# A linear-attention and feed-forward kernel: 96-partition loads and a fixed instruction order in place of scheduled 128-token tiles

## The chip, the cores and the metric

The kernel runs on one core of one Trainium2 chip. The metric is the device time of one execution in microseconds (us), the median of the runs. Profiles are of one execution each, and times inside a profile count from the start of its span. "Matmul" is one TensorE instruction; ACT is ScalarE, DVE is VectorE, POOL is GpSimd, SP is the engine whose queue issues the DMAs, and PEld is the loading of stationary operands.

## The reference

Eight batches, eight heads, 576 tokens, head size 64. Attention without a score matrix feeds a feed-forward block that has no nonlinearity besides one product:

```python
q_s = exp(q - max) / sum over d          # per token and head
k_s = exp(k - max) / sum over tokens     # per head and channel
kv  = einsum('bhsd,bhse->bhde', k_s, v)
x   = einsum('bhsd,bhde->bhse', q_s, kv) # then (b, s, h*64): 4608 tokens x 512
a, b = x @ w1, x @ w2                    # 512 -> 1024 each
out = ((a * b) @ w3) @ w_out             # 1024 -> 1024 -> 512
```

Both kernels fold `w3 @ w_out` into one 1024 x 512 matrix first ("the fold"), so a chunk of 512 tokens costs 64 matmuls in the first stage (a and b, 8 groups of 8) and 32 in the second stage, all with 512 columns. There are 9 chunks. Attention of a batch must be done before the chunks that use its tokens.

## The kernel before

Tokens are loaded in tiles of 128 (four, and one of 64), so that each DMA moves runs of 64 floats, 256 bytes. Every tile gets its own exponential, reduction, normalisation on GpSimd, and one transpose per pair of heads:

```python
for st in range(N_ST):                       # 5 token tiles
    nc.sync.dma_start(out=q32[:ns], in_=q[b, :, s0:s0 + ns, :].transpose([1, 0, 2]))
    # ... k32, v32 the same way
    nc.scalar.activation(out=eq[:ns], in_=q32[:ns], func=AF.Exp)
    # ... ek, v16, dsum, dsr
    nc.gpsimd.tensor_tensor(out=eqn[:ns], in0=eq[:ns],
                            in1=dsr[:ns, :, None].broadcast_to([ns, H, D]), op=ALU.mult)
for p in range(NPAIR):
    # ... kv matmuls over the 5 tiles, two casts into kv2
    for st in range(N_ST):
        nc.tensor.transpose(tpq[:, st, :ns], eqns[st][:ns, 2*p:2*p+2, :]..., ident[:ns, :ns])
    # ... scale by rc on the way to qsT, then x = kv2.T @ qsT (512 + 64 columns)
```

Weights come through two staging buffers and ACT casts. The order of instructions on each engine is left to the tile scheduler; the program is emitted as whole blocks:

```python
attention_batch(0); load_w12(); attention_batch(1); load_w3o(); attention_batch(2)
for j in range(N_CHUNK):
    ffn_chunk(j)
    if j + 3 < B:
        attention_batch(j + 3)
```

The softmax here doesn't subtract the row's maximum and nothing guards it: scores larger than these inputs give would overflow.

## Time and profile before

| | before |
|---|---|
| time | 317.44 us (316.34 to 318.54) |
| span of the profile | 315.9 us |
| TensorE busy | 84% |
| first second-stage matmul (end of the fold) | 101.9 us |
| period of a chunk with attention (second stages of chunks 3 to 6 start at 162.33, 192.55, 221.78, 252.48) | 30.0 us |
| chunk without attention (second-stage starts at 284.2 and 304.9) | 20.8 us |

From the page of the kernel before: the span in 40 slices (7.9 us each), tenths of busy time, granted TensorE clock, DMA share, and GB/s; then the chain that ended last, by engine and by line.

```profile
PE   0128479398999999999989999988898989999995
PEclk9999999855999999999999999999999999999999
DMA  9995799346999499993695478458844402002003
GB/s 172 218 245 192 224 236 220 114 175 200 227 234 212 135 220 215 259 199 67 182 224 113 100 214 178 91 125 226 166 102 100 149 3 100 33 2 101 33 0 133
...
PE 64%; POOL 9%; ACT 8%; DMA 7%; DVE 5%; issue 3%; SPq 2%; POOLq 0%; DVEq 0%; ACTq 0%
```

The start is poor in TensorE work up to about 70 us, with the DMA engines full in five of nine slices at only 172 to 245 GB/s, and two slices (63 to 79 us) near half clock. After that TensorE looks full. It is not: the profile draws a 512-column matmul 0.38 us long although the next one can start 0.216 us after it, so a gap shorter than the difference is not seen as idle. The waits of TensorE between 130 and 230 us (in all, times, longest):

```profile
PE pt L169 <- POOL eqn L149: 7.2, 12, 1.0
```

Then two extracts of the timeline, each with a single transpose between dense matmuls (start, duration, engine, line, operation, operands); above the second, ACT's copy of x out of the PSUM buffer that the transposes share:

```profile
151.16 0.38 PE L206 MATMUL po<-W3O_579,ab 128*128 128x512 f16 x1
151.38 0.22 PE L169 MATMUL pt<-ident,eqn 128*128 128x128 f16 x1
151.43 0.38 PE L206 MATMUL po<-W3O_580,ab 128*128 128x512 f16 x1
```

```profile
120.50 0.23 ACT L182 ACTIVATE xT_102<-pt 128x64 f16<-128x64 f32 x1
120.44 0.38 PE L206 MATMUL po<-W3O_577,ab 128*128 128x512 f16 x1
120.78 0.22 PE L169 MATMUL pt<-ident,eqn 128*128 128x128 f16 x1
120.84 0.38 PE L206 MATMUL po<-W3O_578,ab 128*128 128x512 f16 x1
```

Dense matmuls start 0.216 us apart. The transpose at 151.38 waited for nothing: 0.27 us lie between the starts of its neighbours, so it cost 0.056 us. The one at 120.78 had 0.40 us between its neighbours, 0.13 us of that a wait, too short for the waits view: ACT freed the single PSUM buffer (`pt`) only at 120.73. Of the twenty single 128-column transposes between dense matmuls from 110 to 255 us, only four cost no more than 0.056 us. Twelve transposes between 130 and 230 us waited up to 1.0 us for GpSimd, and the dense matmuls behind them, for which the trace shows no wait of their own, started 0.06 to 0.13 us later.

### The profile page before, as it was taken

The numbers are of one execution on the slowest core, as the hardware profiler recorded it, in microseconds if no ns is written. First come the engines' busy times: TensorE is split into PE (matmuls) and PEld (weight loads), VectorE is DVE, ScalarE is ACT, GpSimd is POOL, SyncE is SP. The second block draws the span as 40 slices with busy tenths as digits, with TensorE's granted clock in tenths as the row PEclk, the third lists the DMA queues.
The fourth block names the chain that finished last, engine by engine and source line by source line (L and its number), as shares of the span: only waits on it lengthen the run. The fifth ranks groups of instructions, "written<-read, shape, count | busy, mean of one in ns | idle before, by whom it ended". The sixth has DMA issues, their size and how long they took to land.

```text
span 315.9 us, 4080 instructions
## 1 busy us (share of the span) xinstructions
PE 264.9 (84%) x1376; PEld 119.9 (38%) x1376; DVE 147.2 (47%) x364; ACT 133.3 (42%) x249; POOL 66.1 (21%) x104
## 2 busy tenths in 40 slices
PE   0128479398999999999989999988898989999995
PEld 0014024144545454335344434444354335444441
DVE  1234024442444485457546645664465447344342
ACT  3336544454865254245343625344433531430320
POOL 4441022400214212422322242132304240000000
PEclk9999999855999999999999999999999999999999
DMA  9995799346999499993695478458844402002003
GB/s 172 218 245 192 224 236 220 114 175 200 227 234 212 135 220 215 259 199 67 182 224 113 100 214 178 91 125 226 166 102 100 149 3 100 33 2 101 33 0 133
DMA packets 121172, 48.49 MB, mean 154 GB/s; under 512 B 113472, under 2 KB 113472, under 8 KB 121152
## 3 DMA queue, kind: packets, MB, share of 16 engines
q1 hardware_dynamic: 121152, 48.25, 66.3%
q8 instruction: 10, 0.16, 0.2%
q14 instruction: 10, 0.08, 0.1%
HBM read 38.80 MB, written 9.44 MB: 153 GB/s over the span
## 4 chain that ended last, share of the span: by engine, by line
PE 64%; POOL 9%; ACT 8%; DMA 7%; DVE 5%; issue 3%; SPq 2%; POOLq 0%; DVEq 0%; ACTq 0%
PE pab L195 18%; PE po L206 15%; PE pab L190 14%; POOL eqn L149 9%; PE pkv L158 5%; PE pt L169 5%; ACT bsb L199 4%; PE po L119 3%; PE px L178 2%; DMA q_173<-in_q_dram 2%; DVE dsum L144 2%; DMA w_716<-in_moe_w_dram 2%; DMA q_207<-in_q_dram 2%; DMA w_352<-in_moe_w_dram 1%; DVE osb L209 1%
## 5 line engine op out<-in xcount | busy, mean ns | idle before, releaser
L201 DVE TENSOR_TENSOR ab<-pab,bsb 128x512 f16<-128x512 f32 x72 | 49.7, 690 | 79.5 <-ACT bsb L199 78.6
L199 ACT CAST bsb<-pab 128x512 f16<-128x512 f32 x72 | 42.1, 585 | 103.8 <-PE pab L195 103.7
L149 POOL TENSOR_TENSOR eqn<-eq,dsr 128x512 f16<-128x512 f16 (+1 forms) x40 | 41.6, 1041 | 177.6 <-DVE dsr L147 67.1
L169 PE MATMUL pt<-ident,eqn 128*128 128x128 f16 (+1 forms) x160 | 22.8, 233 | 26.8 <-POOL eqn L149 25.8
L209 DVE COPY osb<-po 128x512 f32<-128x512 f32 x36 | 24.8, 690 | 25.6 <-PE po L206 25.4
L206 PEld LDWEIGHTS <-ab 128*128 128x128 f16 x288 | 25.3, 98 | 28.3 <-issue 1.4
L144 DVE TENSOR_REDUCE dsum<-eq 128x8 f32<-128x512 f16 (+1 forms) x40 | 27.1, 676 | 17.9 <-ACT eq L137 17.8
L169 PEld LDWEIGHTS <-eqn 128*128 128x128 f16 (+1 forms) x160 | 14.2, 103 | 53.6 <-POOL eqn L149 41.4
L190 PE MATMUL pab<-xT_102,w_0_3_350 128*128 128x512 f16 x72 | 28.3, 396 | 3.2 <-ACT w_0_3_350 L93 2.6
L190 PE MATMUL pab<-xT_101,w_0_2_342 128*128 128x512 f16 x72 | 28.3, 396 | 1.8 <-ACT w_0_2_342 L93 1.2
L195 PE MATMUL pab<-xT_99,w_1_0_330 128*128 128x512 f16 x72 | 28.2, 392 | 1.1 <-ACT bsb L199 1.1
L195 PE MATMUL pab<-xT_102,w_1_3_354 128*128 128x512 f16 x72 | 28.1, 390 | 1.0 <-ACT w_1_3_354 L93 1.0
L190 PE MATMUL pab<-xT_100,w_0_1_334 128*128 128x512 f16 x72 | 28.3, 396 | 0.6 <-ACT xT_100 L181 0.6
L190 PE MATMUL pab<-xT_99,w_0_0_326 128*128 128x512 f16 x72 | 28.5, 396 | 0.0
L195 PE MATMUL pab<-xT_101,w_1_2_346 128*128 128x512 f16 x72 | 28.1, 390 | 0.3 <-ACT w_1_2_346 L93 0.3
L195 PE MATMUL pab<-xT_100,w_1_1_338 128*128 128x512 f16 x72 | 28.1, 390 | 0.0
L173 DVE TENSOR_SCALAR qsT<-pt,rc 128x512 f16<-128x512 f16 x32 | 15.5, 484 | 16.3 <-PE pt L169 15.9
L158 PEld LDWEIGHTS <-ek 128*128 128x128 f16 (+1 forms) x160 | 13.5, 103 | 22.0 <-ACT ek L139 5.9
L206 PE MATMUL po<-W3O_576,ab 128*128 128x512 f16 x36 | 13.7, 380 | 0.0
L206 PE MATMUL po<-W3O_580,ab 128*128 128x512 f16 x36 | 13.7, 380 | 0.0
L206 PE MATMUL po<-W3O_575,ab 128*128 128x512 f16 x36 | 13.7, 380 | 0.0
L206 PE MATMUL po<-W3O_578,ab 128*128 128x512 f16 x36 | 13.7, 380 | 0.0
(284 smaller groups left out, 392.8 us busy)
## 6 DMA issues: line engine op xcount, KB each, us to landing
out_dram<-osb SPq DMA_DIRECT2D x36, 256.0 KB, 2.6
w_324<-in_moe_w_dram SPq DMA_DIRECT2D x1, 512.0 KB, 5.0
w_328<-in_moe_w_dram SPq DMA_DIRECT2D x1, 512.0 KB, 5.8
w_332<-in_moe_w_dram SPq DMA_DIRECT2D x1, 512.0 KB, 3.3
w_336<-in_moe_w_dram SPq DMA_DIRECT2D x1, 512.0 KB, 3.3
w_340<-in_moe_w_dram SPq DMA_DIRECT2D x1, 512.0 KB, 3.2
w_344<-in_moe_w_dram SPq DMA_DIRECT2D x1, 512.0 KB, 3.4
w_348<-in_moe_w_dram SPq DMA_DIRECT2D x1, 512.0 KB, 3.6
```

The costliest lines, as they stand in the source:

```text
L119: nc.tensor.matmul(wps, lhsT=w3Tf[:, gt * P:(gt + 1) * P], rhs=wosb[gt], start=(gt == 0), stop=(gt == N_FT - 1))
L144: nc.vector.tensor_reduce(out=dsum[:ns], in_=eq[:ns], axis=mybir.AxisListType.X, op=ALU.add)
L149: nc.gpsimd.tensor_tensor(out=eqn[:ns], in0=eq[:ns], in1=dsr[:ns, :, None].broadcast_to([ns, H, D]), op=ALU.mult)
L158: nc.tensor.matmul(kvp[:, 0:129], lhsT=eks[st][:ns, p * P:(p + 1) * P], rhs=v16s[st][:ns, p, 0:129], start=(st == 0), stop=(st == N_ST - 1))
L169: nc.tensor.transpose(tpq[:, st, :ns], eqns[st][:ns, 2 * p:2 * p + 2, :].rearrange("a h d -> a (h d)"), ident[:ns, :ns])
L173: nc.vector.tensor_scalar(out=qsT[:, 0:512], in0=tpq[:, 0:4, :], scalar1=rc, scalar2=None, op0=ALU.mult)
L190: nc.tensor.matmul(pa, lhsT=w1sb[ct][:, fb * P:(fb + 1) * P], rhs=xT[ct][:, t0:t0 + 512], start=(ct == 0), stop=(ct == N_CT - 1))
L195: nc.tensor.matmul(pb, lhsT=w2sb[ct][:, fb * P:(fb + 1) * P], rhs=xT[ct][:, t0:t0 + 512], start=(ct == 0), stop=(ct == N_CT - 1))
L199: nc.scalar.copy(out=bsb, in_=pb)
L201: nc.vector.tensor_tensor(out=ab, in0=pa, in1=bsb, op=ALU.mult)
L206: nc.tensor.matmul(po, lhsT=abT[ft][:, tb * P:(tb + 1) * P], rhs=W3O[ft], start=(ft == 0), stop=(ft == N_FT - 1))
L209: nc.vector.tensor_copy(out=osb, in_=po)
```

## The change

The intent: longer DMA runs, fewer and larger operations, and an order of instructions written by hand. Tokens are taken as 96 partitions x 6 consecutive tokens, so that a run is 1536 bytes and half a batch of q, k or v is one DMA of 576 KB; nine staging slots instead of a few; weights w1 and w2 arrive in column quarters, so that the first groups can start early; the scale moves from q to kv. Attention's PSUM buffers change too: three that all its pieces share, in place of one each for kv, for x and for the transposes (with the end of x); and the weight casts are spread over ACT, VectorE and GpSimd. The output rows are permuted back by the store. The guard `manual_schedule()` keeps every engine in the order in which the program emits.

```diff
+    R = 6
+    SP = S // R                                     # 96 partitions
+    stage = ctx.enter_context(tc.tile_pool(name="stage", bufs=9))
+    def load_qkv(b, which, hf):
+        t = slot([SP, 4, R * D])
+        nc.sync.dma_start(out=t, in_=src[b, 4*hf:4*hf+4].rearrange("h (p r) d -> p h (r d)", r=R))
+    def piece_t(b, p):                              # 6 transposes, one copy
+    def piece_kv(b, g):                             # 12 matmuls; kv2 scaled by rc here
+    def piece_x(b, p):                              # 2 matmuls of 288 columns, ACT copies
+    order = ctx.enter_context(tc.manual_schedule())
 ...
+    elementwise(1, 1)
+    pc = pieces(1)
+    for tb in range(4):
+        s2(0, tb)                                   # second stage of chunk 0, with its stores
+        for f in ((1, 0, 2), (3, 4, 5), (6, 7), (8, 9))[tb]:
+            pc[f]()
+    for which in "kvq":
+        load_qkv(2, which, 1)
+    elementwise(2, 0)                               # k exp, v cast, q exp, reduction, normalisation
+    elementwise(2, 1)
+    for hf in range(2):
+        for which in "kvq":
+            load_qkv(3, which, hf)
+    for j in range(1, N_CHUNK):                     # one piece and one elementwise step
+        for i, (kind, n) in enumerate(seq):         # after each group
+            if kind == "g": s1(j, n)
+            elif j > 1:     s2(j - 1, n)
+            if i < len(pc): pc[i]()
+            if i < len(ew): ew[i]()
+            if i >= 4 and i - 4 < len(ld): load_qkv(j + 3, *ld[i - 4])
 ...
-    for j in range(N_CHUNK):
-        ffn_chunk(j)
-        if b < B: attention_batch(b)
```

## The prediction

> **What bounds it now.** TensorE. In the timeline's last two chunks, where only FFN is left, one 512-token chunk (96 matmuls of 512 columns) takes 20.8 us (second-stage starts at 284.2 and 304.9), 0.216 us per matmul. The Trainium skill ("TensorE: Matmul & The Clock Gate", Back-to-back issue gap) gives about 216 ns for N=512; the trace agrees. FFN needs 9 x 20.8 = 187 us; folding w3 into w_out 64 x 0.216 + 64 transposes = about 18 us; attention about 4.5 us per batch. Together about 241 of the 316 us span; some 75 us are lost, in two places:
> - Start, 0 to 102 us. The first second-stage matmul is at 101.8 us in the chain. Batch 0's 256-byte packets keep the DMA engines full (share 1.0 to 1.3) for 180 to 220 GB/s; 4 KB weight rows move 158 GB/s at share 0.54, so about 290 GB/s when full. The Trainium skill ("DMA: Bandwidth & Descriptors", Specifications) asks for at least 512 B per transfer; the trace agrees. Weights come through two staging buffers: each load waits for an ACT cast (1.05 us) and its own 3.3 us to landing. From 60 to 80 us the granted clock is 0.55 to 0.6.
> - Steady state. A chunk with attention takes about 29 us against 20.8 + 4.5. The waits view shows TensorE held by the GpSimd normalisation (7.2 us between 130 and 230), because transposes stand singly in TensorE's order ahead of matmuls that were ready.
>
> **What the change does.**
> - 1536-byte runs, 6 loads per batch instead of 15, nine staging slots: batch 0 (3.5 MB) lands by about 14 us, w1/w2 by 28, w_out by 35, w3 by 49 (estimate at 290 to 300 GB/s). Chunk 0's first stage starts at about 22 us and runs dense (14 us); the fold, 2.3 us per row block, ends at about 57 us instead of 101.
> - Hand order: attention pieces come as bursts between dense groups, normalised a chunk ahead, so TensorE should hardly wait. Each chunk with attention: 20.8 + about 5.6 us.
> - Added: 24 + 24 small matmuls per batch instead of 20 + 20, about 0.1 us each; two 288-column matmuls instead of 512 + 64: about +1 us per batch on TensorE. More output DMAs (split at 96 rows), off the chain. DVE per chunk (12 x 0.69, 4 reductions of about 0.95, copies) about 16 us of 26; ACT about 15; GpSimd about 11: none binds. Moving the scale to kv saves small DVE operations, nothing on the chain.
>
> **Sum.** Fold ends at 57; second stage of chunk 0 with attention 1: 12.5 plus 1 to 2 us waiting for batch 1's loads, to 71; chunk 1 first stage with attention 2: 19.4, to 90; chunks 2 to 6: 5 x 26.4, to 222; chunks 7, 8: 41.6; last second stage 6.9; eviction and output DMA 4 (as now). About 275 us of span, plus 1.5 (time over span now): **276 us, range 264 to 290**. Faster by over 2%: 0.96; within 2%: 0.03; slower: 0.01.
>
> **Right if:** first second-stage matmul at 53 to 62 us; first-stage start at 19 to 26; chunk period with attention 25.5 to 28; GpSimd nearly gone from the chain, TensorE over 80% of it; no 256-byte packets, 280 GB/s or more at the start; last two chunks unchanged.
>
> **Wrong if:** in-order ACT or DVE delays first-stage evictions (exponentials of 0.85 us queue before them), so that three PSUM buffers run out and the period is 28 or more; GpSimd contends with DVE; the start is limited by casts or slots, not bandwidth, and the fold ends after 65 us; half clock after stalls in the fold; or small matmuls cost more than 0.1 us in bursts.

## The result

| | before | after |
|---|---|---|
| time | 317.44 us | 291.35 us (290.51 to 292.19) |
| ratio | | 0.916 (0.908 to 0.924) |
| first stage of chunk 0 | scattered, from 24.8 us | dense, from 27.2 us |
| first second-stage matmul | 101.9 us | 70.4 us |
| period of a chunk with attention | 30.0 us | 24.14 us |
| last second stage with store | about 11 us | about 11.5 us |

Ratios here are the mean time of one kernel's fast runs over that of the other's in the same rounds, so they are not quite the ratios of the medians quoted beside them. The change is faster by 8%, but 15 us short of the forecast of 276.

The same lines of the page of the changed kernel (slices of 7.3 us):

```profile
PE   0218997739693399999999999999999999999993
PEclk9999999998888579999999999999999999999999
DMA  7999999990139999949946965971121112121124
GB/s 182 254 326 391 357 351 282 261 250 15 41 97 236 256 256 256 228 118 220 280 129 156 257 149 128 261 208 38 48 62 38 36 47 64 36 73 38 55 76 121
...
PE 79%; DMA 8%; ACT 5%; DVE 3%; issue 1%; SPq 1%; DVEq 0%; ACTq 0%
```

From about 106 us on TensorE has no hole. Before that there are deep ones around 62 us and from 87 to 102 us, a smaller one around 76 us, reduced clock in several slices, and, at 65 to 87 us, three slices in which the DMA engines do almost nothing (15, 41, 97 GB/s) in a kernel that is waiting for data.

Extracts of the chain of the changed kernel in order of time, from the end of the fold on (start, length, what):

```profile
61.07 1.57 ACT ek L111 x2
62.65 1.47 ACT eq L120 x2
64.11 0.94 ACT w_611 L232
65.10 1.03 PE att L235 x8
...
86.21 1.19 ACT ek L111 x2
87.40 9.72 DMA st<-in_q_dram
97.20 1.58 ACT eq L120 x2
99.29 1.86 PE pab L204 x4
```

Two stops stand out. In the fold, TensorE's last transposes wait for a cast of w3 (w_611) that stands behind four exponentials on ACT. In chunk 1, TensorE waits until 99.29 us for something that begins with a load. ACT's own timeline and SP's show how (the bracket is the engine's idle time before the row and what ended it):

```profile
86.07 1.59 ACT L111 ACTIVATE ek<-st 96x768 f16<-96x768 f32 x2
87.55 1.58 ACT L120 ACTIVATE eq<-st 96x768 f16<-96x768 f32 x2
92.55 1.58 ACT L111 ACTIVATE ek<-st 96x768 f16<-96x768 f32 x2 [3.43 <-DMA st<-in_k_dram]
97.20 1.58 ACT L120 ACTIVATE eq<-st 96x768 f16<-96x768 f32 x2 [3.07 <-DMA st<-in_q_dram]
98.68 0.56 ACT L201 CAST a_880<-pab 128x512 f16<-128x512 f32 x1
...
76.37 9.92 SPq L224 DMA_DIRECT2D out_dram<-osb  x8
86.39 0.37 SPq L78 DMA_DIRECT2D st<-in_k_dram  x1
86.88 0.41 SPq L78 DMA_DIRECT2D st<-in_v_dram  x1
87.40 0.42 SPq L78 DMA_DIRECT2D st<-in_q_dram  x1
```

The first-stage copy a_880 needs nothing but a matmul that ended at about 87 us. It runs at 98.68 us, because eight exponentials of batch 2 come before it on ACT, four of them wait for loads, and those loads were issued only at 86.4 us, after the eight stores of chunk 0's second stage had gone through the same SP queue. The Trainium skill ("TensorE: Matmul & The Clock Gate", the specification table's row Engine queue depth) calls the queues of ScalarE, VectorE and GpSimd strict FIFO; this trace agrees, with a ready copy of 0.56 us held for some 11 us.

Two more losses of chunk 1 do not stand out in the chain. TensorE waited 3.9 us, until 91.38 us, for GpSimd's normalised tile of batch 2: the exponentials before it (86.07 and 87.55) were emitted only after chunk 0's second stage, although their loads had landed by 66.8 us (experiment 6 moves them, and this wait goes). And after the stops TensorE ran slowly: from 91.9 to 105.3 us its 512-column matmuls started 0.43 us apart in place of 0.216 (granted clock 0.50 from 94 to 102 us), which cost an estimated 3.6 us, by these distances.

### The profile page after: what moved, and what is told of

Same layout as the page of the kernel before. It is cut to its first block, busy times and chain, and to the rows that moved or that the text cites. A ratio compares the mean times of both kernels' runs of the same rounds, so it can differ in the third digit from the quotient of the medians.

```text
span 290.4 us, 3985 instructions
## 1 busy us (share of the span) xinstructions
PE 245.5 (85%) x1440; PEld 125.1 (43%) x1440; DVE 140.0 (48%) x268; ACT 124.3 (43%) x217; POOL 79.2 (27%) x64
## 2 busy tenths in 40 slices
DMA packets 31443, 48.49 MB, mean 167 GB/s; under 512 B 2240, under 2 KB 24768, under 8 KB 31424
## 4 chain that ended last, share of the span: by engine, by line
PE 79%; DMA 8%; ACT 5%; DVE 3%; issue 1%; SPq 1%; DVEq 0%; ACTq 0%
PE pab L204 22%; PE pab L198 21%; PE po L215 21%; DMA st<-in_q_dram 8%; PE po L243 5%; PE att L152 4%; PE att L180 3%; PE att L169 2%; ACT eq L120 2%; ACT ek L111 1%; PE att L235 1%; DVE ds L134 1%; SPq L78 1%; DVE osb L218 0%; ACT w_542 L232 0%
## 5 line engine op out<-in xcount | busy, mean ns | idle before, releaser
L138 POOL TENSOR_TENSOR eqn<-eq,dr 96x768 f16<-96x768 f16 x32 | 46.8, 1470 | 98.9 <-DVE dr L136 57.5
L134 DVE TENSOR_REDUCE ds<-eq 96x12 f32<-96x768 f16 x32 | 30.0, 936 | 44.2 <-ACT eq L120 44.1
L215 PEld LDWEIGHTS <-abT 128*128 128x128 f16 x288 | 27.6, 99 | 30.5 <-issue 1.1
L218 DVE TENSOR_SCALAR osb<-po 128x512 f32<-128x512 f32 x36 | 24.8, 688 | 27.2 <-PE po L215 26.2
L120 ACT ACTIVATE eq<-st 96x768 f16<-96x768 f32 x32 | 26.4, 843 | 11.8 <-DMA st<-in_q_dram 11.8
L111 ACT ACTIVATE ek<-st 96x768 f16<-96x768 f32 x32 | 25.8, 843 | 8.5 <-DMA st<-in_k_dram 8.5
L169 PE MATMUL att<-ident,eqn 96*128 96x96 f16 x192 | 14.8, 219 | 7.7 <-POOL eqn L138 7.7
L152 PEld LDWEIGHTS <-ek 96*128 96x128 f16 x192 | 14.5, 108 | 13.9 <-ACT ek L111 7.0
L215 PE MATMUL po<-W3O_93,abT 128*128 128x512 f16 x36 | 13.9, 386 | 0.0
L215 PE MATMUL po<-W3O_96,abT 128*128 128x512 f16 x36 | 13.9, 386 | 0.0
L215 PE MATMUL po<-W3O_95,abT 128*128 128x512 f16 x36 | 13.9, 385 | 0.0
L215 PE MATMUL po<-W3O_94,abT 128*128 128x512 f16 x36 | 13.9, 385 | 0.0
L215 PE MATMUL po<-W3O_97,abT 128*128 128x512 f16 x36 | 13.7, 381 | 0.0
L215 PE MATMUL po<-W3O_98,abT 128*128 128x512 f16 x36 | 13.6, 379 | 0.0
L215 PE MATMUL po<-W3O_99,abT 128*128 128x512 f16 x36 | 13.6, 379 | 0.0
L215 PE MATMUL po<-W3O_100,abT 128*128 128x512 f16 x36 | 13.6, 379 | 0.0
L204 PE MATMUL pab<-xT_71,w_0_85 128*128 128x512 f16 x18 | 7.3, 404 | 5.9 <-ACT a_880 L201 5.9
```

Source lines behind the costliest of these rows:

```text
L111: nc.scalar.activation(out=ek.rearrange("p r h d -> p h r d"), in_=t[:, o:o + 2].rearrange("p h (r d) -> p h r d", r=R), func=AF.Exp)
L120: nc.scalar.activation(out=eq.rearrange("p r h d -> p h r d"), in_=t[:, o:o + 2].rearrange("p h (r d) -> p h r d", r=R), func=AF.Exp)
L134: nc.vector.tensor_reduce(out=ds, in_=eq, axis=AX.X, op=ALU.add)
L138: nc.gpsimd.tensor_tensor(out=eqn.rearrange("p r h d -> p (r h) d"), in0=eq, in1=dr[:, :, None].broadcast_to([SP, 2 * R, D]), op=ALU.mult)
L152: nc.tensor.matmul(kvp[:, pp, :].rearrange("p (h e) -> p h e", h=2), lhsT=ek[:, r].rearrange("p h d -> p (h d)"), rhs=v16buf[b % 2][:, 2 * ...
L169: nc.tensor.transpose(pt[:, r, :], eqn[:, r].rearrange("p h d -> p (h d)"), ident[:SP, :SP])
```

## The experiments

Theory A: the shortfall is made by order, not by work: what was emitted ahead on an in-order engine (ACT first of all) waited for data, and ready work stood behind it. Rivals: GpSimd's normalisation or the DMA rate set the pace whatever the order; TensorE's own fixed order costs it; the data of the fold come too slowly.

### 1. Loads issued ahead of the stores

```diff
+    for which in "kvq":
+        load_qkv(2, which, 1)
     elementwise(1, 1)
     ... second stage of chunk 0 ...
-    for which in "kvq":
-        load_qkv(2, which, 1)
```

> One edit to the changed kernel: the second-half loads of batch 2 (k, v, q) are issued ahead of chunk 0's second stage, so that the DMA queue does not stand behind that stage's output stores. Theory A (chunk 1 stood because these loads were issued at 86.4 us, behind the stores, and ACT's in-order exponentials waited for them while first-stage evictions queued behind): the DMA share between 65 and 86 us rises from about 0.15, the TensorE wait of 5.9 us on the first-stage copy ends some 6 us sooner, time falls by 5 to 9 us, to about 283 to 286. Rival B (GpSimd's normalisation, 2.9 us per pair of heads groups, or the DMA rate itself is what held chunk 1): time stays within 2 us of 291.

Measured: 284.8 us, ratio 0.898 (0.8935 to 0.9025), as theory A expected. The three loads were issued at 62.9 to 65.6 us instead of 86.4 to 87.8. The wait of 5.9 us on the copy is gone: TensorE's largest wait after the fold is now 3.9 us, for GpSimd. It is the wait at 91 us of the changed kernel, which these loads do not touch. Some of the other moved: batch 3's q exponentials, next in ACT's order, still waited 2.25 us for their load in the middle of chunk 1.

### 2. ACT's order changed, loads as late as before

```diff
     elementwise(2, 0)
-    elementwise(2, 1)
 ...
+            if j == 1 and i == 3:
+                elementwise(2, 1)
```

> Loads as in the changed kernel, but the exponentials and normalisation of batch 2's second half are moved in program order from before chunk 1 to after the third first-stage group of chunk 1. Theory A (ACT in order is what turned late loads into a TensorE stop): the copy that waited until 98.7 us runs at about 89, the single wait of 5.9 us goes, and only the pieces that truly need the late data wait; time falls by 4 to 7 us, to 284 to 287, although the loads land as late as before. Rival B' (the data are late, so whatever is done TensorE waits for them): 291 within 2 us.

Measured: 295.44 us, ratio 0.9339 (0.9282 to 0.9396): slower than the changed kernel (0.916, in other rounds; the intervals do not overlap), and the expected time failed. The timeline of ACT in this run:

```profile
89.11 0.58 ACT L201 CAST a<-pab 128x512 f16<-128x512 f32 x1
99.09 0.84 ACT L111 ACTIVATE ek<-st 96x768 f16<-96x768 f32 x1 [9.40 <-DMA st<-in_k_dram]
```

The first copy did run at 89.1 us. But the next thing in ACT's order was the first exponential of batch 3, whose load had been issued even later, and ACT stood 9.40 us for it. Moving one waiting block only put another at the head of the queue. So the copy's delay was ACT's order, as theory A says, and the cure is not to move one block: everything placed ahead of ready work must have its data by then.

### 3. Casts of w3 one block ahead

```diff
+    w3_c(0); w3_c(1)                      # casts alone, split from the transposes
     w3_t(0)
     for ft in range(N_FT):
         if ft + 1 < N_FT: w3_t(ft + 1)
+        if ft + 2 < N_FT: w3_c(ft + 2)
         w3_m(ft)
```

> Fold of w3: the fp16 cast of row block n+2 is emitted before the matmuls of block n, so that on ACT it stands ahead of the copy of the result and ahead of batch 1's exponentials. Theory C (TensorE's three waits of 1.6, 1.6 and 4.5 us in the fold come from ACT's order: cast behind copy, and cast behind four exponentials): these three waits vanish, the first second-stage matmul moves from 70.4 to about 63 us, but part is lost again because batch 1's exponentials and chunk 1's late loads do not move as much; time falls by 3 to 7 us, to 284 to 288. Rival (w3 arrives too slowly, DMA-bound): the waits stay, named for the DMA, time 291 within 1 us.

Measured: 283.76 us, ratio 0.8941 (0.8891 to 0.8991). TensorE's waits for casts in the fold fell from 8.1 us in all to 0.3. A new one of 3.7 us took part of it: the copy of the last transposes on VectorE stood behind two reductions that waited for the exponentials. The wait of chunk 1 is still there, 5.1 us. The w3 data were not late.

### 4. The order left to the scheduler

```diff
-    order = ctx.enter_context(tc.manual_schedule())
```

> The changed kernel without the hand order: same layout, loads, casts and arithmetic, but the instruction order is left to the scheduler that ordered the kernel before. If the hand order gives the steady state its 24.1 us per chunk with attention (before 29), this run shows periods of 27 us or more there, single transposes waiting for GpSimd, and a time of 300 to 315 us. If the layout gives it, the period stays near 24 and the time is 280 to 295.

Measured: 272.73 us, ratio 0.8604 (0.8563 to 0.8644). The period is that of the second reading, but the time met neither: without the hand order the kernel is not slower but faster by some 18 us, and faster than either of the two kernels compared. The period of a chunk with attention is 24.14 us here too (second-stage starts at 120.45, 144.60, 168.74). The list of DMA instructions is the same, line for line. TensorE's waits between 42 and 120 us, in the changed kernel and then in this run (in all, times, longest):

```profile
PE pab L204 <- ACT a_880 L201: 5.9, 1, 5.9
PE att L235 <- ACT w_611 L232: 4.5, 1, 4.5
PE att L169 <- POOL eqn L138: 3.9, 1, 3.9
PE att L180 <- DVE qsT L172: 2.4, 1, 2.4
```

```profile
PE att L169 <- POOL eqn L138: 5.8, 9, 1.1
PE po L243 <- DVE w3T L237: 1.0, 1, 1.0
PE pab L204 <- ACT a L201: 0.2, 1, 0.2
```

On ACT the scheduler put the w3 casts ahead of the copies and of the exponentials, and the exponentials of batches 2 and 3 between the first-stage copies. Its mean clock was 0.998 against 0.964: the slow stretch that followed the stops of the changed kernel is not there. The final stretch of 40 second-stage matmuls starts at 258.5 us instead of 277.2.

### 5. Which engine's order it was

Two runs keep the hand order on some engines only:

```diff
-    tc.manual_schedule()
+    tc.manual_schedule(engines={PE, DVE, Pool, SP})     # ACT free
+    tc.manual_schedule(engines={PE, Pool, SP})          # ACT and DVE free (second run)
```

> The changed kernel with the hand order kept on TensorE, VectorE, GpSimd and the DMA queue (their instruction lists are the same, line for line) and only ScalarE's order left to the scheduler; all engines free gave 272.7. Theory A (ScalarE's fixed order, in which exponentials that wait for loads and casts that wait for copies stand ahead of first-stage copies, costs the 15 us by which the forecast was short): at least two thirds of the 18.7 us come back, time 272 to 279; the 5.9 us wait in chunk 1 and the three waits in the fold go. Rival D (the order on TensorE or VectorE, transposes ahead of ready matmuls and reductions ahead of evictions, costs it): time 285 to 291.

> Hand order kept on TensorE, GpSimd and the DMA queue; ScalarE and VectorE free. With ScalarE alone free the time was 280.8, and TensorE still stood 7.0 us once for VectorE's kv copy, behind reductions that waited for late exponentials. If VectorE's order is the other part of the 18.7 us, the time falls to 271 to 276 and that wait goes; if TensorE's or GpSimd's order is, it stays at 279 to 282.

Measured: 280.83 us with ACT free, ratio 0.8831 (0.8794 to 0.8867); 279.31 us with ACT and DVE free, ratio 0.8779 (0.8735 to 0.8822). In the profiles the last 40 matmuls start at 266.9 and 264.4 us, against 277.2 (all fixed) and 258.5 (all free). So ACT's order is the largest single part, 10.3 of 18.7 us, less than the two thirds expected. Freeing VectorE after it adds 2.5 us in these profiles but 1.5 us in the medians, and the intervals of the two ratios overlap, so its part is not clear of the noise; its wait of 7.0 us did go, replaced by others, and the time is that of the reading in which TensorE's or GpSimd's order is the rest. The last 5.9 us come only when those two are free as well (the SP queue too, but its list is the same in all these runs). In the second run TensorE waits 7.9 us in two pieces for GpSimd's normalisation, with transposes at the head of its fixed order. Theory A holds in its general form (a fixed order with waiting work ahead), not in its narrow one (ACT alone), and the rival about TensorE's order is partly right. Since TensorE and GpSimd were not freed separately, which of the two owns the rest is open.

### 6. The hand order repaired

```diff
+    casts of w3 one block ahead, as in experiment 3
+    load_qkv(2, *, 1) and load_qkv(3, *, 0) ahead of chunk 0's second stage
-    elementwise(2, 0); elementwise(2, 1)  # one block ahead of chunk 1
+    batch 2, half 0: exponentials after the 3rd and 4th second-stage groups of chunk 0
+    batch 2, half 1: one step after each of chunk 1's first groups, batch 3's steps after it
```

> Hand order on all engines, repaired by what the first runs showed: casts of w3 one block ahead; loads of batch 2's second half and batch 3's first half issued ahead of chunk 0's second stage; batch 2's exponentials spread over the end of that stage and over chunk 1's groups instead of standing in one block of eight ahead of chunk 1. Theory A: no wait of TensorE over 2 us between 40 and 110 us, time 268 to 276, as the free order. If fixed order as such is the cost and not what stood where, it stays above 280.

Measured: 272.52 us, ratio 0.8577 (0.8538 to 0.8617), the same as the free order of experiment 4. So what stood where, not a fixed order as such, made nearly all of the 18 us. The two runs differ in more than order, though: this one also issues loads early. The free order with early loads (experiment 8, 270.8 us) is 1.7 us faster still, at the edge of the intervals, so that a small cost of this fixed order is not excluded. One wait over 2 us was left, 3.7 us in the fold for VectorE's copy, so that the expectation of none failed by one.

### 7. What the loads can move

The changed kernel loads q, k and v at about 255 GB/s and weights at about 390, both with the DMA engines full. Two windows of it (us; then busy time and count of PE, PEld, DVE, ACT, POOL; granted clock; DMA share; GB/s), one with q, k, v in flight and one with weights:

```profile
5.00:10.00 5.00, 0.03 (x1) 0.13 (x2) 0.00 (x0) 1.58 (x2) 1.46 (x1) 1.00 1.09 253
25.00:30.00 5.00, 4.67 (x18) 1.96 (x17) 2.05 (x4) 4.21 (x9) 0.39 (x1) 1.00 1.07 393
```

A kernel of loads alone, in phases that do not overlap:

```python
phase("head", 96, 4, 384)    # partitions, runs per partition, floats per run
phase("flat", 96, 6, 256);  phase("flat", 128, 3, 384); phase("w", 128, 4, 256)
phase("head", 64, 4, 576);  phase("flat", 96, 1, 1536); phase("flat", 128, 1, 1152)
```

> Wrong result on purpose: only loads, in seven phases of six loads each that do not overlap, then zeros are stored. Six loads of 576 KB (512 KB for the weight phase) as: 96 partitions x 4 runs of 1536 B (as in the changed kernel), 96 x 6 runs of 1 KB, 128 x 3 runs of 1536 B, 128 x 4 runs of 1 KB (weight quarters as in the changed kernel), 64 x 4 runs of 2304 B, 96 x 1 run of 6 KB, 128 x 1 run of 4.5 KB. In the changed kernel the 96-partition loads move about 255 GB/s with the engines full, the weights about 390. Theory P (the number of partitions sets it): all 96-partition phases near 255 GB/s, both multi-run 128-partition phases 350 to 400, 64 partitions 170 to 220. Rival R (run length or the order of runs in HBM sets it): phases of equal run length have equal rates, whatever the partitions.

Each load is followed by a small copy on VectorE that waits for it, so their distance is the time of one load. The first and last of the phase of 96 x 1536 B, then of 128 x 1536 B:

```profile
5.56 0.15 DVE L56 COPY z<-ph 96x1 f32<-96x1 f32 x1 [4.17 <-DMA ph<-in_q_dram]
17.33 0.15 DVE L56 COPY z<-ph 96x1 f32<-96x1 f32 x1 [1.86 <-DMA ph<-in_v_dram]
...
37.02 0.15 DVE L56 COPY z<-ph 128x1 f32<-128x1 f32 x1 [4.09 <-DMA ph<-in_q_dram]
45.09 0.15 DVE L56 COPY z<-ph 128x1 f32<-128x1 f32 x1 [1.33 <-DMA ph<-in_v_dram]
```

Five loads of 589,824 bytes in 11.77 us are 251 GB/s; in 8.07 us, 365 GB/s. In the same way:

| partitions | run | GB/s |
|---|---|---|
| 64 | 2304 B | 215 |
| 96 | 1024 B | 275 |
| 96 | 1536 B | 251 |
| 96 | 6144 B | 278 |
| 128 | 1024 B (weights) | 315 (with one gap; 344 or more between the others) |
| 128 | 1536 B | 365 |
| 128 | 4608 B | 368 |

The number of partitions sets the rate far more than the run length: theory P, though the weights phase missed its figure, and 96 partitions range from 251 to 278. The Trainium skill ("SBUF — State Buffer", Door 1: The DMA port swizzle) counts the ports that the partitions reach; by its table 96 partitions reach all 16, half of them with half the load. If that imbalance were the limit, loads starting alternately at partition 0 and at 32 should even it out. A second such kernel tried it:

```python
phase(96, 4, 384, (0,)); phase(96, 4, 384, (32,)); phase(96, 4, 384, (0, 32))   # start partitions
phase(64, 4, 576, (0,)); phase(64, 4, 576, (64,)); phase(64, 4, 576, (0, 64))
```

> Wrong result on purpose: only loads of 576 KB, six per phase. 96 partitions starting at 0; starting at 32; alternately at 0 and 32; 64 partitions starting at 0; at 64; alternately at 0 and 64. Theory (which partitions are written decides how many ways into the memory are used, and alternating starts spreads the load evenly): alone 240 to 260 GB/s for 96 and 205 to 215 for 64 partitions at either start; alternating 64s rises to 340 or more, alternating 96s to 300 or more. Rival (each load is bound by its own number of partitions or rows per engine): alternating changes nothing.

Measured, five loads each, as above: 253, 275 and, alternating, 257 GB/s for 96 partitions; 217, 208 and, alternating, 214 GB/s for 64. Alternating gives no more than one start alone, as the rival expected; whether loads of one queue overlap enough for the test to bite was not measured, so the mechanism stays open. For the forecast it is enough that 96-partition loads move 250 to 278 GB/s, not the 290 to 300 that were read from 128-partition weight loads.

### 8. Early loads, and q first, in free order

```diff
-    order = ctx.enter_context(tc.manual_schedule())
+    load_qkv(2, *, 1) and load_qkv(3, *, *) ahead of chunk 0's second stage
     # second run only:
-    batch 0 loaded k, v, q, k, v, q; elementwise per half
+    batch 0 loaded q, q, k, v, k, v; all q exponentials and normalisations first
```

> All engines in free order, and loads of batch 2's second half and batch 3 issued ahead of chunk 0's second stage. In the free-order run the DMA engines idle from 61 to 81 us and are full, at 258 GB/s, from 81 to 122 us, while TensorE waits. Theory (in chunks 0 to 2 the free order is bound by late loads): share of DMA from 61 to 81 us rises, time falls by 3 to 8 us, to 265 to 270. Rival (GpSimd and VectorE chains bind there, or the output stores now come late and hold the buffers): 272 within 2 us or slower.

> The fastest so far (free order, early loads, 270.8) with batch 0 loaded as q, q, k, v, k, v and its q exponentials and normalisations emitted first. Theory S (the start is bound by the last q load, which lands at 17.7 us at 255 GB/s, and by the chain exponential, reduction, GpSimd, transpose behind it): the first dense first-stage matmuls come 3 to 6 us sooner, the time falls by 2 to 5 us, to 266 to 269. Rival (the start is bound by total bytes, weights included, or the gain is lost to later loads): 270 to 272.

Measured: 270.8 us with early loads, ratio 0.8502 (0.8463 to 0.8542). The DMA engines no longer idle at 61 to 81 us (255 to 262 GB/s there, after 77 to 205), but that gained only about 2 us, less than the 3 to 8 expected: GpSimd's normalisation still holds TensorE in six short waits between 42 and 115 us (4.3 us in all, 5.8 us in nine waits before), and the free order had already worked around most of the late loads.

With q first as well: 265.09 us, ratio 0.8341 (0.8285 to 0.8397). The fold's first transposes start at 37.5 us instead of 43.0, and theory S holds (the time is even 0.9 us under its range): the start was bound by the last q load and by the chain behind it. This run beats both kernels: it is the changed kernel without the hand order, with two groups of loads moved and batch 0's q work emitted first. A row of its page:

```profile
GB/s 182 256 314 385 411 417 331 264 258 262 269 261 294 229 249 248 250 274 118 118 264 205 132 189 276 136 49 40 41 42 40 40 44 76 43 40 53 69 80 120
```

From the second slice to the eighteenth (6.6 to 118 us) the DMA engines move 229 to 417 GB/s without a pause, against the hole at 65 to 87 us of the changed kernel.

### 9. Layout or interleaving

```diff
-    one attention piece after each group of a chunk
+    s1(j, *); s2(j, *); then elementwise and pieces of batch j + 2 in one block   # free order
```

> Free order, new layout and loads, but from chunk 1 on emitted as in the kernel before: a whole chunk, then the whole attention of a later batch, instead of attention pieces between groups. If the layout (fewer, larger operations; 6 loads) is what took the period of a chunk with attention from 29 to 24.1 us, the period stays under 25 and the time is 270 to 280. If the interleaving does it, single transposes wait for GpSimd again, the period is 26 us or more and the time 282 to 300.

Measured: 275.37 us, ratio 0.8652 (0.8618 to 0.8686), first reading confirmed. The period is 24.54 us (second stages start at 172.14, 196.68 and 221.22), against 24.14 with interleaving and 30.0 before, and the longest wait of TensorE between 130 and 230 us is 0.4 us. So the layout, with what came with it, brings 5.5 us of the 5.9 us per chunk, and interleaving the rest and some of the start. What came with it was not taken apart: fewer and larger operations on GpSimd, nine staging slots, and three shared PSUM buffers in place of single ones. In the timeline of the changed kernel a chunk's attention comes in bursts:

```profile
107.77 0.86 PE L152 MATMUL att<-v_0_75,ek 96*128 96x130 f16 x12
108.47 0.42 PE L169 MATMUL att<-ident,eqn 96*128 96x96 f16 x6
108.73 0.38 PE L198 MATMUL pab<-xT_71,w_2_83 128*128 128x512 f16 x1
```

Twelve kv matmuls take 0.70 us to the next start, 58 ns each; six transposes 0.26 us, 43 ns each. That is no cheaper than before: there a single kv matmul or transpose that waited for nothing took 56 to 57 ns. At these rates, with 0.216 us for each long matmul of x, a batch of the kernel before is an estimated 3.2 us of TensorE work (20 x 0.057 + 20 x 0.056 + 4 x 0.216, and a little for the four short ones), but a chunk with attention took 9.2 us more than one without. So about 6 us per chunk were waits, and these went: between 121 and 218 us the waits view of the changed kernel is empty. The largest part named in the trace is GpSimd's normalisation; the single PSUM buffers, as at 120.78 us above, are a rival that no run tested. One normalised tile now frees six transposes at once, which fits the bursts.

## Why the prediction was right or wrong

The direction was right, the time was 15 us short. Its sum, term by term, in the profile's span:

| term | forecast, us | measured, us | difference |
|---|---|---|---|
| start of chunk 0's first stage | 22 | 27.2 | +5.2 |
| first stage of chunk 0 | 14 | 15.4 | +1.4 |
| fold | 21 | 27.8 | +6.8 |
| second stage of chunk 0 with attention 1 | 14 | 15.1 | +1.1 |
| first stage of chunk 1 with attention 2 | 19.4 | 31.3 | +11.9 |
| chunks 2 to 6 | 132 | 120.7 | -11.3 |
| chunks 7, 8 and the end | 52.5 | 52.9 | +0.4 |

- **What bounds the kernel before: right.** TensorE in steady state, the start by DMA and weight staging, single transposes held by GpSimd.
- **"Chunk 1 first stage with attention 2: 19.4": wrong, the largest miss.** The sum added TensorE's work and took for granted that a hand order has no waits. Late loads behind stores and exponentials ahead of ready copies (5.9 us of waiting), exponentials emitted too late for the first transposes (3.9 us) and the half clock after these stops (an estimated 3.6 us; "half clock after stalls" stood under "Wrong if", for the fold) made it 31.3 us. The prediction named the danger (in-order ACT delaying evictions) but put it in the steady state, where it did not occur; it belongs where loads are late. Experiments 1, 4, 5 and 6 show that order did it: with the same layout and a repaired order, the time is 272.5 us, inside the stated range.
- **"The fold, 2.3 us per row block": mis-sized.** The matmuls do take that long when nothing waits, but three casts stood behind copies and exponentials on ACT (8.1 us with the first small one, experiment 3).
- **"Estimate at 290 to 300 GB/s": wrong.** That rate was read from 128-partition loads of 4 KB rows; the new 96-partition loads move 251 GB/s (experiment 7), so batch 0 landed at 17.7 us, not 14, and the chain behind it began later. The check "280 GB/s or more at the start" failed with it.
- **"Each chunk with attention: 20.8 + about 5.6": too high.** It measured 20.8 + 3.4. The 0.1 us per small matmul is what the start of the kernel before shows (kv matmuls 0.11 us apart at 22.6 us, where 512-column ones too start 0.43 us apart); in the steady state they take 43 to 58 ns (and 0.12 us for the two of 288 columns). By luck, this error of 11.3 us hid some two fifths of the others, 26.8 us together.
- **"Hand order ... so TensorE should hardly wait", as the cause of the shorter period: wrong cause.** Free order has the same 24.14 us (experiment 4), and even block emission has 24.54 (experiment 9). The layout and what came with it did.
- **The named checks:** the first second-stage matmul (70.4 us, named 53 to 62) and the first-stage start (27.2, named 19 to 26) failed high, the period (24.14, named 25.5 to 28) failed low. The fold's end at 70.4 us also met the condition "the fold ends after 65 us" under "Wrong if".
- **Right as stated:** loads without 256-byte packets (2,240 packets under 512 bytes remain, 16 for each of the 140 DMAs); GpSimd gone from the chain's top; last chunks unchanged; VectorE, ACT and GpSimd not binding in steady state (15.2, 13.2 and 8.7 us busy of 24.1). TensorE's share of the chain was 79%, just under the 80% named.

Where the gain came from is also not where it was expected. At 162.3 us the kernel before has 547 of its 512-column matmuls left in the records and 3.9 batches of attention to go; the changed one has 519 and 3 at 163.4 us. The difference, 28 matmuls and 0.9 batches, is worth an estimated 9 us at the changed kernel's cost of a batch (3.4 us) and 14 us at the other's (9.2 us), less the 1.1 us by which it was counted later. So after all stops of its start it is 8 to 13 us ahead, although its fold had ended 31 us sooner, and some half to two thirds of the 25.5 us of span is earned after that point, where attention no longer makes TensorE wait.

## What to carry to other kernels

A fixed instruction order must be checked like a schedule: for every instruction placed ahead of ready work on an in-order engine, ask when its data land, and for every load, what stands before it in the issuing queue; a repaired fixed order and a scheduler's order came within 2 us of each other here, and a fixed order that is wrong cost 18 us. When a rewrite combines a layout with an order, try the layout with the order taken away before believing in either. Take the rate of a load from loads of the same number of partitions, and the cost of a small matmul from the steady state, from one that waited for nothing: a gap between starts can hold a wait that the waits view does not list.

## What the Trainium skill lacked or had wrong

- "DMA: Bandwidth & Descriptors" (Specifications; Measured) and "SBUF — State Buffer" (Door 1: The DMA port swizzle) have no rate for 96 partitions, and the second page's count of ports (16, as for 128 partitions) does not give the rate found. Measured: 251 to 278 GB/s for 96 partitions, against 365 to 368 for 128 with the same total per load, with runs of 1 to 6 KB.
- "TensorE: Matmul & The Clock Gate" (Back-to-back issue gap) gives about 81 ns per matmul for sustained pairs of weight load and 128-column matmul, and about 131 ns at 512 columns. Measured here: 58 ns with 130 columns and 43 ns with 96 columns (96 rows of weights), and 216 ns with 512 columns; all three agree with an estimate by the page's formula for the isolated gap (57, 43 and 216 ns), and not with its sustained figures.
- No page joins the parts that it states (strict FIFO engines, semaphore waits on the engine that issues a DMA) into the case that cost much here: a load queue shared with stores delays a load by waiting for the stores' data (loads that could go at about 63 us, as experiment 1 shows, were issued at 86.4 us).
